# Spectral filter plus max-out experts on one core: wide exchange transfers through memory, filter rows doubled by TensorE, other loads held back in the opening

## The chip, the cores and the metric

One core of one Trainium2 chip runs the whole program. The metric is the device time of one execution in microseconds (us); runs of one kernel agree within about 1%. The profile of a kernel is one execution; its span is about 2 us shorter than the time.

Ratios are computed from the mean time of one kernel's fast runs over that of the other's of the same rounds, so a ratio is not quite the ratio of the medians that are quoted beside it.

## The reference

```python
# x: (8, 3072, 256) float32; filt_r, filt_i: (1537, 256); w1, w2: (256, 1024); w_out: (1024, 256)
X = np.fft.rfft(x, axis=1)
y = np.fft.irfft(X * (filt_r + 1j * filt_i)[None], n=3072, axis=1)   # a filter along the sequence
t = y.reshape(8 * 3072, 256)
out = np.maximum(t @ w1, t @ w2) @ w_out                             # the experts
```

## The kernel before

The transform of 3072 points is split as 128 x 24, and a batch of 3072 x 256 goes through these steps:

1. `gen_f1`: 12 matmuls with a 128 x 128 table (`C1`), evicted by ScalarE into `at` and stored to memory as `ad`.
2. `ad` is read back in another order as the *frequency tile* `bt` (96 partitions x 32 t x 256). This is the first exchange through memory.
3. `gen_f2`: for each of 16 pairs of t, a matmul with `U`, the product with the filter rows `F` on VectorE (`pqt`), four matmuls back (`pz`), eviction by ScalarE into `zt`, a store to `zd` (the *spectrum store*).
4. `zd` is read back as `zr` (128 partitions): the second exchange, called *read-back* below.
5. `s4` finishes the inverse transform; `moe_h` and `moe_o` are the experts. The maximum is rewritten as a ReLU of a difference of weights; that weight preparation (`prep_w`) is done once.

The experts of batch b run on TensorE while `gen_f2` of batch b+1 and `gen_f1` of batch b+2 are mixed in step by step. Before that can begin there is an *opening* that has nothing to hide behind: `gen_f1` and `gen_f2` of batch 0, `prep_w`, `gen_f1` of batch 1.

```python
    def copy_f(t0, t1):                       # the filter rows are needed twice, on partitions 0-47 and 48-95
        for ri in range(2):
            nc.sync.dma_start(out=F[48:96, ri, t0:t1], in_=F[0:48, ri, t0:t1])

    def load_f0():                            # 18 transfers of 1 to 12 rows, on the SyncE queue
        for ri, f in enumerate((filt_r, filt_i)):
            for dr in range(2):
                for mm, row0 in enumerate((0, 96) if dr == 0 else (32, 64)):
                    for q in range(2):
                        ...
    # ... (cut)
    # end of gen_f1: the frequency tile, 8 transfers over 24 partitions
                for h in range(2):
                    for rs in range(4):
                        src = ad[32 * rs + 16 * h:32 * rs + 16 * h + 16].rearrange("t n d -> n t d")
                        nc.sync.dma_start(out=bt_[24 * rs:24 * rs + 24, 16 * h:16 * h + 16], in_=src)
    # ... (cut)
    # gen_f2: the spectrum store, and at its end the read-back, 12 transfers over 32 partitions
            if g % 2 == 1:
                nc.sync.dma_start(out=zd[:, 2 * g - 2:2 * g + 2], in_=zt)
        # ...
        for g in list(range(2, 16)) + [0, 1]:
        # ...
        for c in range(3):
            for rs in range(4):
                src = zd[24 * rs + 8 * c:24 * rs + 8 * c + 8].rearrange("n t d -> t n d")
                nc.sync.dma_start(out=zr_[32 * rs:32 * rs + 32, 8 * c:8 * c + 8], in_=src)
    # ... (cut)
    # the opening
    drain(gen_f1(0))
    copy_f(1, 16)
    copy_f(16, 32)
    load_f0()
    load_w()
    for c in range(12):
        load_x(1, c)
    sines_u(uu, mk)
    tables_pe()
    f2 = gen_f2(0)
    # ... 16 steps of f2, prep_w(), drain(f2), drain(gen_f1(1)), loads of batch 2, s4(0)
```

(`load_f0` issues 18 transfers in all. The prediction and the expectations below say 28 small loads; that was a miscount.)

## Time and profile before

| | before |
|---|---|
| time, median (range) | 615.5 us (610.87 to 616.45) |
| first filter product (`pqt`) | 55.3 us |
| weight preparation begins (`w2b`) | 82.2 us |
| first expert matmul (`ph`) | 111.7 us |
| seventh tile's gap | 16.3 us, against 11.1 for its like six tiles later |
| from the sixth output store to the last | 416.2 us |

The page of the kernel before, its span and the mean busy share of the transfer engines in 40 equal slices (tenths):

```profile
span 613.5 us, 10246 instructions
DMA  8997529656976596658767785778336822261111
```

The stretches view: for each stretch its length, the busy us of TensorE (PE), its weight loads (PEld), VectorE (DVE), ScalarE (ACT), GpSimd (POOL), with the number of instructions in brackets, then the clock granted to TensorE, the transfer engines' share (the time of all packets over that of 16 engines; it can exceed 1), and GB/s:

```profile
0.00:20.00 20.00, 7.42 (x13) 1.27 (x13) 14.87 (x50) 8.99 (x15) 15.63 (x35) 1.00 0.93 155
20.00:40.00 20.00, 5.37 (x39) 3.83 (x39) 4.00 (x7) 9.57 (x20) 8.22 (x16) 1.00 1.22 201
40.00:60.00 20.00, 4.49 (x20) 3.87 (x21) 4.28 (x4) 1.19 (x2) 0.28 (x1) 1.00 0.87 167
60.00:80.00 20.00, 15.55 (x68) 12.25 (x67) 13.95 (x14) 5.45 (x11) 0.00 (x0) 1.00 0.48 158
80.00:100.00 20.00, 11.24 (x56) 7.03 (x54) 4.68 (x5) 9.08 (x16) 4.76 (x9) 0.92 0.53 99
100.00:120.00 20.00, 9.41 (x44) 5.11 (x45) 2.82 (x5) 7.99 (x15) 0.00 (x0) 0.57 0.82 205
200.00:220.00 20.00, 20.00 (x157) 15.29 (x156) 13.70 (x15) 13.32 (x25) 4.27 (x8) 1.00 0.65 154
```

The last line is the state of nearly all of the run: TensorE busy all the time, transfers at 0.65. The six lines above it are the opening, in which no engine is full. Who holds it up is in the waits view (engine and tile that waited, for what, us in total, times, longest):

```profile
DVE pqt L346 <- DMA F<-F: 23.5, 1, 23.5
ACT at L310 <- DMA ad<-at: 17.1, 3, 14.4
PE px L343 <- DMA bt__271<-ad: 15.3, 1, 15.3
ACT zt L335 <- DMA zd<-zt: 11.9, 2, 11.6
PE px L343 <- DMA bt__1412<-ad: 3.4, 1, 3.4
```

Read in order of time these are one chain: the frequency tile is late, then the doubled filter rows, then ScalarE has no free store buffer because stores are not issued, then the same again for the next transform. Why stores are not issued shows in the timeline of SyncE, which issues most transfers in program order (start, us, what, how many):

```profile
27.10 16.50 SPq L318 DMA_DIRECT2D bt__271<-ad  x8
43.72 7.84 SPq L102 DMA_DIRECT2D F<-F  x4
62.87 4.58 SPq L117 DMA_DIRECT2D F_96<-in_filt_i_dram  x6
68.62 22.49 SPq L337 DMA_DIRECT2D zd<-zt  x8
93.45 10.04 SPq L357 DMA_DIRECT2D zr__665<-zd  x12
103.83 7.65 SPq L312 DMA_DIRECT2D ad<-at  x6
```

The first product begins at 55.3 and ScalarE evicts it at 57.6, but the first store is issued at 68.6, behind the small filter loads; the stores of the next transform are issued at 103.8, behind twelve read-backs.

The output stores (start us, first column) mark the tiles. A tile is stored one tile later, so the time from the fifth store to the sixth is what TensorE spends on the seventh tile's first matmuls and the sixth's last ones; it is called the *seventh tile's gap* here. It is 16.3 us. The gaps repeat every six tiles, so its like is the gap of the thirteenth tile, 11.1 us:

```profile
174.56 0.54 POOL L416 DMA_DIRECT2D out_dram<-ot  x1 [7.72 <-DVE ot L412]
190.88 0.54 POOL L416 DMA_DIRECT2D out_dram<-ot  x1 [14.70 <-DVE ot L412]
242.51 0.53 POOL L416 DMA_DIRECT2D out_dram<-ot  x1 [7.73 <-DVE ot L412]
253.62 0.54 POOL L416 DMA_DIRECT2D out_dram<-ot  x1 [9.50 <-DVE ot L412]
```

### The profile page before, as it was taken

The page shows a single profiled execution, that of the slowest core. Times are in us where ns is not written, and L with a number is a line of the kernel's source. Part 1 is how long each engine was busy: PE and PEld are TensorE (multiplying, and loading weights), DVE is VectorE, ACT ScalarE, POOL GpSimd, SP SyncE. Part 2 cuts the span into 40 slices and gives each one's busy share as a digit, 9 for nine tenths or more (in the row PEclk, how much of TensorE's full clock was granted, in tenths as well). Part 3 has the DMA queues.
Part 4 walks back from the last instruction along what each step waited for, and adds up shares of the span by engine and source line. Part 5 has one row for each costly group of instructions (what it writes and reads, how often), then busy time and mean ns, then how long its engine had stood idle before and what let it go on. Part 6 is the DMA issues. An engine that isn't in the chain of part 4 may idle for free.

```text
span 613.5 us, 10246 instructions
## 1 busy us (share of the span) xinstructions
PE 536.0 (87%) x4008; PEld 395.0 (64%) x4008; DVE 335.0 (55%) x430; ACT 329.5 (54%) x588; POOL 86.0 (14%) x167
## 2 busy tenths in 40 slices
PE   3403771799979999999999999999999999999995
PEld 0203550477657777777777777777777777777774
DVE  8203740288337664666466637663667377734342
ACT  3801161566536754765476556765666455555541
POOL 8430002011111111111121102110000000000000
PEclk9999996699989999999999999999999999999998
DMA  8997529656976596658767785778336822261111
GB/s 140 208 188 148 180 62 219 171 123 169 225 182 156 134 220 198 153 152 183 212 150 179 163 218 145 183 156 233 125 112 161 225 83 78 74 185 70 69 69 69
DMA packets 90784, 94.62 MB, mean 154 GB/s; under 512 B 7360, under 2 KB 71504, under 8 KB 90592
## 3 DMA queue, kind: packets, MB, share of 16 engines
q1 hardware_dynamic: 66720, 54.17, 33.6%
q0 software_dynamic: 24016, 39.81, 28.5%
q8 instruction: 31, 0.51, 0.3%
q14 instruction: 17, 0.14, 0.1%
HBM read 56.72 MB, written 50.33 MB: 174 GB/s over the span
## 4 chain that ended last, share of the span: by engine, by line
PE 43%; issue 34%; DMA 12%; SPq 4%; POOL 3%; ACT 1%; DVE 1%; POOLq 0%; ACTq 0%
PE ph L385 14%; PE po L410 13%; PE po L405 3%; DMA xb<-in_x_dram 3%; PE pz L333 3%; PE px L343 3%; PE pz L334 3%; DMA Wo<-in_moe_w_out_dram 2%; DMA zd<-zt 2%; SPq L117 2%; POOL out_dram L416 2%; PE pa L309 2%; PE py L369 2%; DMA ad<-at 2%; DMA zr__665<-zd 1%
## 5 line engine op out<-in xcount | busy, mean ns | idle before, releaser
L410 PE MATMUL po<-Wo,gt 128*128 128x256 bf16 x1536 | 230.4, 273 | 0.0
L390 ACT ACTIVATE gt<-ph 128x512 bf16<-128x512 f32 x288 | 170.7, 593 | 100.4 <-PE ph L385 97.0
L346 DVE TENSOR_TENSOR pqt<-px,F 96x1024 bf16<-96x1024 f32 x128 | 156.0, 1219 | 107.6 <-PE px L343 83.6
L410 PEld LDWEIGHTS <-gt 128*128 128x128 bf16 x1536 | 150.2, 98 | 58.2
L335 ACT ACTIVATE zt<-pz 96x512 bf16<-96x512 f32 x128 | 75.3, 593 | 111.4 <-PE pz L334 87.9
L412 DVE COPY ot<-po 128x512 f32<-128x512 f32 x96 | 66.4, 692 | 75.8 <-PE po L410 75.8
L416 POOL DMA_DIRECT2D out_dram<-ot x48 | 25.8, 537 | 452.9 <-DVE ot L412 418.1
L385 PEld LDWEIGHTS <-Wd 128*128 128x128 bf16 x768 | 74.0, 99 | 19.5 <-issue 4.8
L310 ACT ACTIVATE at<-pa 128x512 bf16<-128x512 f32 x96 | 55.8, 597 | 54.0 <-PE pa L309 33.9
L388 DVE TENSOR_SCALAR gt<-ph 128x512 bf16<-128x512 f32 x96 | 65.5, 682 | 28.7 <-PE ph L385 28.7
L333 PE MATMUL pz<-pqt,VP 96*96 96x256 bf16 x256 | 67.9, 289 | 11.0 <-DVE pqt L346 10.7
L334 PE MATMUL pz<-pqt,VQ 96*96 96x256 bf16 x256 | 68.2, 290 | 0.0
L87 POOL DMA_DIRECT2D xb<-in_x_dram x96 | 51.4, 558 | 66.4 <-PE pa L309 50.4
L343 PEld LDWEIGHTS <-U 96*96 96x96 bf16 x256 | 32.5, 134 | 24.6 <-issue 22.9
L309 PE MATMUL pa<-xb,C_58 128*128 128x512 bf16 x96 | 38.3, 409 | 10.3 <-DMA xb<-in_x_dram 9.4
L334 PEld LDWEIGHTS <-VQ 96*96 96x96 bf16 x256 | 33.4, 130 | 13.2 <-issue 12.7
L333 PEld LDWEIGHTS <-VP 96*96 96x96 bf16 x256 | 33.7, 131 | 1.8 <-DVE pqt L346 1.1
L343 PE MATMUL px<-bt__271,U 96*96 96x256 bf16 x32 | 9.8, 416 | 18.3 <-DMA bt__271<-ad 15.3
L309 PEld LDWEIGHTS <-C_58 128*128 128x128 bf16 x96 | 9.5, 99 | 18.3 <-issue 7.5
L369 PE MATMUL py<-G_59,zr__665 128*128 128x128 bf16 x48 | 4.6, 248 | 14.6 <-ACT at L310 14.6
L369 PEld LDWEIGHTS <-zr__665 128*128 128x128 bf16 x48 | 3.9, 112 | 15.9 <-DMA zr__665<-zd 9.8
L374 DVE TENSOR_SCALAR y__760<-py 128x512 bf16<-128x512 f32 x1 | 0.7, 692 | 19.9 <-PE py L369 19.9
(334 smaller groups left out, 565.8 us busy)
## 6 DMA issues: line engine op xcount, KB each, us to landing
out_dram<-ot POOLq DMA_DIRECT2D x48, 512.0 KB, 3.9
xb<-in_x_dram POOLq DMA_DIRECT2D x96, 128.0 KB, 6.0
ad<-at SPq DMA_DIRECT2D x48, 256.0 KB
zd<-zt SPq DMA_DIRECT2D x64, 192.0 KB
bt__271<-ad SPq DMA_DIRECT2D x8, 192.0 KB
zr__665<-zd SPq DMA_DIRECT2D x12, 128.0 KB
bt__727<-ad SPq DMA_DIRECT2D x8, 192.0 KB
zr__1295<-zd SPq DMA_DIRECT2D x12, 128.0 KB
```

The source lines that it names most:

```text
L309: TE.matmul(pa, C1, xb[b, c], start=True, stop=True)
L310: S.activation(at[:, 2 * (c % 2):2 * (c % 2) + 2], pa, AF.Copy)
L333: TE.matmul(pz[:, i], VP[:, 2 * g + i], pqt[:, 0, i], start=True, stop=False)
L334: TE.matmul(pz[:, i], VQ[:, 2 * g + i], pqt[:, 1, i], start=False, stop=True)
L335: S.activation(zt[:, 2 * (g % 2):2 * (g % 2) + 2], pz, AF.Copy)
L343: TE.matmul(px[:, i], U[:, 2 * g + i].rearrange("p a b -> p (a b)"), bt_[:, 2 * g + i], start=True, stop=True)
L346: V.tensor_tensor(pqt, px.rearrange("p (o i) d -> p o i d", o=1).to_broadcast([QP, 2, 2, D]), F[:, :, 2 * g:2 * g + 2], OP.mult)
L385: TE.matmul(ph, Wd[:, dc, 128 * j:128 * j + 128], y_[:, dc].rearrange("p a b -> p (a b)"), start=(dc == 0), stop=(dc == 1))
L388: V.tensor_scalar(gt[tt][:, j], ph, 0.0, None, OP.max)
L390: S.activation(gt[tt][:, j], ph, AF.Relu)
L410: TE.matmul(p_, g_[:, jj, 128 * n:128 * n + 128], Wo[:, jj], start=False, stop=(jj == 7))
L412: V.tensor_copy(ot[tt][:, n - 1:n + 1], po[tt])
```

## The change

Its intent: lay out both exchanges so that they take few transfers over many partitions; take the doubling of the filter rows and the many small filter loads off the transfer queue; and hold back loads that the opening does not need. It also begins the products with t = 16 (whose filter rows are now loaded first), reads the spectrum back in two halves, the first of them in the middle of the tile, and gives four of batch 0's 16 products to GpSimd. For batch 0 it also lets two products wait for their matmuls back instead of one, and finishes the tile before the weight preparation. Cut to its core:

```diff
-        G.dma_start(out=t_, in_=src[:, 2 * c:2 * c + 2, :])        # 12 loads of 128 KB per batch
+        G.dma_start(out=t_, in_=src[:, 4 * c:4 * c + 4, :])        # 6 of 256 KB
 ...
-    def copy_f(t0, t1):
+    def copy_f(t0, t1, engine):
         for ri in range(2):
-            nc.sync.dma_start(out=F[48:96, ri, t0:t1], in_=F[0:48, ri, t0:t1])
+            for t in range(t0, t1, 2):
+                n = min(2, t1 - t)
+                pf = ps.tile([QP, 2, D], FP32, tag="ps", name="pf")
+                TE.matmul(pf[:, 0:n], DM, F[0:48, ri, t:t + n], start=True, stop=True)
+                ...  # evicted by VectorE or ScalarE into F[:, ri, t:t + n]
 ...  # load_f0: 4 loads at the start and 3 transfers later, instead of 18 small loads
-        S.activation(C1, uc.rearrange("p a b c -> p (a b c)"), AF.Sin, bias=zero, scale=TWO_PI)
+        S.activation(C1.rearrange("p (c a b) -> p a b c", a=2, b=2), uc, AF.Sin, bias=zero, scale=TWO_PI)
 ...
                 for h in range(2):
-                    for rs in range(4):
-                        src = ad[32 * rs + 16 * h:32 * rs + 16 * h + 16].rearrange("t n d -> n t d")
-                        nc.sync.dma_start(out=bt_[24 * rs:24 * rs + 24, 16 * h:16 * h + 16], in_=src)
+                    src = ad.rearrange("(t r) n d -> (r n) t d", r=4)[:, 16 * h:16 * h + 16]
+                    nc.sync.dma_start(out=bt_[:, 16 * h:16 * h + 16], in_=src)
 ...
-                nc.sync.dma_start(out=zd[:, 2 * g - 2:2 * g + 2], in_=zt)
+                nc.sync.dma_start(out=zd[2 * g - 2:2 * g + 2].rearrange("t p d -> p t d"), in_=zt)
+            if g == 15:
+                zr[b] = zrpool.tile([128, N2, D], BF16, tag="zr", name="zr")
+                read_z(1)
+            if g == 1:
+                read_z(0)
+        def read_z(h):
+            nc.sync.dma_start(out=zr[b][64 * h:64 * h + 64],
+                              in_=zd[16 * h:16 * h + 16].rearrange("t (r n) d -> (t r) n d", r=4))
-        for g in list(range(2, 16)) + [0, 1]:
+        for n, g in enumerate(list(range(8, 16)) + list(range(2, 8)) + [0, 1]):
 ...
+            if b == 0 and n in (1, 5, 9, 12):
+                E = G        # the product on GpSimd, from a copy in SBUF made by ScalarE
 ...  # the opening
     drain(gen_f1(0))
-    copy_f(1, 16)
-    copy_f(16, 32)
-    load_f0()
+    copy_f0()
     load_w()
-    for c in range(12):
-        load_x(1, c)
+    copy_f(16, 32, V)
     sines_u(uu, mk)
     tables_pe()
+    copy_f(2, 16, S)
+    copy_f(1, 2, S)
     f2 = gen_f2(0)
 ...  # inside the 16 steps: the last weight's load after step 1, batch 1's loads after steps 5 and 12
```

More of the change, by code (lines that the diff above doesn't have):

```diff
@@ L69 @@
     dram = ctx.enter_context(tc.tile_pool(name="dram", bufs=2, space=bass.MemoryType.DRAM))
-    xpool = ctx.enter_context(tc.tile_pool(name="xpool", bufs=16))
+    xpool = ctx.enter_context(tc.tile_pool(name="xpool", bufs=8))
     apool = ctx.enter_context(tc.tile_pool(name="apool", bufs=3))
@@ L76 @@
     pso = ctx.enter_context(tc.tile_pool(name="pso", bufs=2, space=bass.MemoryType.PSUM))
+    zrpool = ctx.enter_context(tc.tile_pool(name="zrpool", bufs=2))
     setup = ExitStack()
@@ L84, in load_x @@
     def load_x(b, c):
-        t_ = xpool.tile([128, 2, D], BF16, tag="xb", name="xb")
+        t_ = xpool.tile([128, 4, D], BF16, tag="xb", name="xb")
         src = x[b].rearrange("(p n) d -> p n d", n=N2)
-        G.dma_start(out=t_, in_=src[:, 2 * c:2 * c + 2, :])
+        G.dma_start(out=t_, in_=src[:, 4 * c:4 * c + 4, :])
         xb[b, c] = t_
@@ L98, in load_f @@
                 G.dma_start(out=F[24 * dr:24 * dr + 24, ri, t0:t1], in_=fsrc(f, row0, 64, 24, dt, t1 - t0))
-    def copy_f(t0, t1):
+    def copy_f(t0, t1, engine):
         for ri in range(2):
-            nc.sync.dma_start(out=F[48:96, ri, t0:t1], in_=F[0:48, ri, t0:t1])
+            for t in range(t0, t1, 2):
+                n = min(2, t1 - t)
+                pf = ps.tile([QP, 2, D], FP32, tag="ps", name="pf")
+                TE.matmul(pf[:, 0:n], DM, F[0:48, ri, t:t + n], start=True, stop=True)
+                if engine is V:
+                    V.tensor_copy(F[:, ri, t:t + n], pf[:, 0:n])
+                else:
+                    S.activation(F[:, ri, t:t + n], pf[:, 0:n], AF.Copy)
     F0 = init.tile([QP, 2, D], FP32)
@@ L109, in load_f0, with copy_f0 @@
             for dr in range(2):
-                for mm, row0 in enumerate((0, 96) if dr == 0 else (32, 64)):
-                    for q in range(2):
-                        p0 = 48 * q + 24 * dr + mm
-                        if p0 == 48:
-                            nc.sync.dma_start(out=F0[48:49, ri], in_=f[1536:1537, :])
-                            nc.sync.dma_start(out=F0[50:72:2, ri], in_=fsrc(f, 128, 128, J - 1, 1, 1))
-                        else:
-                            nc.sync.dma_start(out=F0[p0:p0 + 23:2, ri], in_=fsrc(f, row0, 128, J, 1, 1))
+                src = bass.AP(f.tensor, f.offset + 32 * dr * D, [[128 * D, J], [(96 - 64 * dr) * D, 2], [1, D]])
+                nc.sync.dma_start(out=F0[24 * dr:24 * dr + 24, ri], in_=src)
+    def copy_f0():
+        nc.sync.dma_start(out=F0[49:96], in_=F0[1:48])
+        nc.sync.dma_start(out=F0[48:49, 1], in_=filt_i[1536:1537, :])
+        nc.sync.dma_start(out=F0[48:49, 0], in_=filt_r[1536:1537, :])
+    DM = init.tile([48, QP], BF16)
     SW = init.tile([QP, QP], BF16)
@@ L121 @@
     zero = init.tile([128, 1], FP32)
+    V.memset(zero, 0.0)
     pid = init.tile([128, 1], FP32)
@@ L140 @@
            allow_small_or_imprecise_dtypes=True)
-    for c in range(12):
+    for c in range(6):
         load_x(0, c)
+    V.memset(DM, 0.0)
+    V.memset(I128, 0.0)
+    V.memset(SW, 0.0)
+    for b0 in (0, 48):
+        G.affine_select(out=DM, in_=DM, pattern=[[-1, QP]], compare_op=OP.not_equal,
+                        fill=1.0, base=b0, channel_multiplier=1)
+    G.affine_select(out=I128, in_=I128, pattern=[[-1, 128]], compare_op=OP.not_equal,
+                    fill=1.0, base=0, channel_multiplier=1)
+    G.affine_select(out=SW, in_=SW, pattern=[[-1, QP]], compare_op=OP.not_equal,
+                    fill=1.0, base=-48, channel_multiplier=1)
+    G.affine_select(out=SW, in_=SW, pattern=[[-1, QP]], compare_op=OP.not_equal,
+                    fill=-1.0, base=48, channel_multiplier=1)
     def table_c():
@@ L147, in table_c @@
         V.memset(kc[:, 1, 0, 0:1], 64.0)
-        V.memset(zero, 0.0)
         p128 = init.tile([128, 1], FP32)
@@ L157, in table_c @@
         V.tensor_tensor(uc, uc, rc, OP.subtract)
-        S.activation(C1, uc.rearrange("p a b c -> p (a b c)"), AF.Sin, bias=zero, scale=TWO_PI)
+        S.activation(C1.rearrange("p (c a b) -> p a b c", a=2, b=2), uc, AF.Sin, bias=zero, scale=TWO_PI)
     def tables_u():
-        V.memset(I128, 0.0)
-        G.affine_select(out=I128, in_=I128, pattern=[[-1, 128]], compare_op=OP.not_equal,
-                        fill=1.0, base=0, channel_multiplier=1)
-        V.memset(SW, 0.0)
-        G.affine_select(out=SW, in_=SW, pattern=[[-1, QP]], compare_op=OP.not_equal,
-                        fill=1.0, base=-48, channel_multiplier=1)
-        G.affine_select(out=SW, in_=SW, pattern=[[-1, QP]], compare_op=OP.not_equal,
-                        fill=-1.0, base=48, channel_multiplier=1)
         pq = pid[0:QP]
@@ L277, in load_w, with load_wo @@
         nc.sync.dma_start(out=w2f, in_=moe_w2.rearrange("(c p) j -> p c j", p=128))
+    def load_wo():
         G.dma_start(out=Wo, in_=moe_w_out.rearrange("(c p) j -> p c j", p=128))
@@ L308, in gen_f1 @@
             pa = ps.tile([128, 2, D], FP32, tag="ps")
-            TE.matmul(pa, C1, xb[b, c], start=True, stop=True)
+            TE.matmul(pa, C1, xb[b, c // 2][:, 2 * (c % 2):2 * (c % 2) + 2], start=True, stop=True)
             S.activation(at[:, 2 * (c % 2):2 * (c % 2) + 2], pa, AF.Copy)
@@ L323, in gen_f2 @@
         bt_ = bt[b]
-        zd = dram.tile([QP, T, D], BF16, tag="zd")
+        zd = dram.tile([T, QP, D], BF16, tag="zd")
         pend = []
@@ L345, in gen_f2 @@
             pqt = pqpool.tile([QP, 2, 2, D], BF16, tag="pq")
-            V.tensor_tensor(pqt, px.rearrange("p (o i) d -> p o i d", o=1).to_broadcast([QP, 2, 2, D]),
+            E = V
+            if b == 0 and n in (1, 5, 9, 12):
+                E = G
+                xs = init.tile([QP, 2, D], FP32, tag="xs", name="xs")
+                S.activation(xs, px, AF.Copy)
+                px = xs
+            E.tensor_tensor(pqt, px.rearrange("p (o i) d -> p o i d", o=1).to_broadcast([QP, 2, 2, D]),
                             F[:, :, 2 * g:2 * g + 2], OP.mult)
             pend.append((g, pqt))
-            if len(pend) > 1:
+            if len(pend) > (2 if b == 0 else 1):
                 s3(*pend.pop(0))
             yield
-        s3(*pend.pop(0))
-        zr_ = zrpool.tile([128, N2, D], BF16, tag="zr")
-        for c in range(3):
-            for rs in range(4):
-                src = zd[24 * rs + 8 * c:24 * rs + 8 * c + 8].rearrange("n t d -> t n d")
-                nc.sync.dma_start(out=zr_[32 * rs:32 * rs + 32, 8 * c:8 * c + 8], in_=src)
-        zr[b] = zr_
+        while pend:
+            s3(*pend.pop(0))
         yield
@@ L421, in drain @@
             pass
+    load_f0()
     table_c()
+    load_f(16, 32)
     load_f(1, 16)
-    load_f(16, 32)
     uu, mk = tables_u()
     drain(gen_f1(0))
-    copy_f(1, 16)
-    copy_f(16, 32)
-    load_f0()
+    copy_f0()
     load_w()
-    for c in range(12):
-        load_x(1, c)
+    copy_f(16, 32, V)
     sines_u(uu, mk)
     tables_pe()
+    copy_f(2, 16, S)
+    copy_f(1, 2, S)
     f2 = gen_f2(0)
-    for g in range(16):
-        if g == 13:
+    for n in range(16):
+        if n == 14:
             fix_f()
         next(f2)
+        if n == 1:
+            load_wo()
+        if n in (5, 12):
+            for c in range(3):
+                load_x(1, c + 3 * (n // 12))
+    drain(f2)
     prep_w()
     setup.close()
-    zrpool = ctx.enter_context(tc.tile_pool(name="zrpool", bufs=2))
     ypool = ctx.enter_context(tc.tile_pool(name="ypool", bufs=3))
@@ L446 @@
     opool = ctx.enter_context(tc.tile_pool(name="opool", bufs=2))
-    drain(f2)
     drain(gen_f1(1))
-    for c in range(12):
+    for c in range(6):
         load_x(2, c)
@@ L472 @@
                     next(f1, None)
-                c = (step - 3) // 2 - (5 if b == 0 else 0)
-                if b + 3 < B and step % 2 and 0 <= c < 12:
+                c = (step - 3 - (12 if b == 0 else 0)) // 4
+                if b + 3 < B and step % 4 == 3 and 0 <= c < 6:
                     load_x(b + 3, c)
```

## The prediction

> **What bounds the kernel now.** Two regimes. From about 187 to 604 us TensorE is busy in every 20 us stretch (stretches view: 20.00 of 20.00, clock 1.00); six output tiles take about 62.7 us (output stores). No transfer is on that path. From 0 to 111.7 us (first expert matmul, timeline) TensorE is mostly idle: 7.4, 5.4, 4.5, 15.6, 11.2, 9.4 us per 20 us. That opening is a chain of transfers. The waits view and the timeline name the links:
> - TensorE waits 15.3 us for the first frequency tile (46.0); VectorE idles 23.5 us until the filter rows doubled by SBUF-to-SBUF transfers arrive: first filter product at 55.3.
> - 28 small filter loads hold the transfer queue from 51.6 to 67.5. The first spectrum store is issued at 68.6; the store buffers fill, ScalarE waits 11.6 us, and the last pz is at 90.2.
> - Weight prep costs about 7 us (82.2 to 89.4), then 12 read-backs hold the queue from 93.4 to 103.5; the stores behind them cost ScalarE 14.4 us and TensorE 14.6 us.
> - Later, TensorE waits 3.4 us for a frequency tile at 174.5; that output tile takes 16.3 us against the usual 11.8: about 4.5 us lost.
> Transfers are saturated in the opening (share 0.93, then 1.22).
>
> **What the change does.** It removes 1.5 MB of doubling copies and 28 tiny loads. The second batch's and the last weight's loads (3.1 and 1.0 MB read) leave the window of the first tile. A frequency read becomes 2 transfers over 96 partitions instead of 8 over 24; a spectrum read-back 2 over 64 instead of 12 over 32. The Trainium skill (DMA: Bandwidth & Descriptors, "Why a DMA increments its semaphore by 16 and not by 1") takes as engine count the largest number up to 16 dividing the outer sizes: 12 for 24, 16 for 96. No view here shows engines singly. Rows of 512 B move from the spectrum read to its write.
> It adds 32 doubling matmuls, evicted by VectorE and ScalarE (0.69 and 0.59 us like those of that size: 11 and 9.5 us). Four products go to GpSimd; the Trainium skill (GPSIMD Engine Reference, "Elementwise — side-by-side cycle accounting") has it about 2x slower, so an estimated 2.5 us against VectorE's 1.22, hidden by the deeper pipeline. No run shows that yet.
>
> **New opening (estimates).** Frequency tile in at about 31; filter rows land at 20 to 28; doubling, table swaps (4.5 us VectorE) and doubling again are serial in TensorE's order: first product at about 41. Sixteen products at about 1.3 us (TensorE alone takes 1.28): last pz near 63. Weight prep 7, the second batch's transform 7 to 8 (12 evictions of 0.6), read-back hidden behind them: first expert matmul near 79 instead of 111.7. That is 33 us, all on the critical path, plus about 4 of the stall at 174.5. The rest stays.
>
> **Predicted: 579 us, range 569 to 594.** Chances: faster by over 2% 0.95, within 2% 0.04, slower by over 2% 0.01.
>
> **What would show it.** First product at 38 to 46 us; no filter-copy wait on VectorE; spectrum stores issued as they are made; first expert matmul at 73 to 87 us; no TensorE wait at the third batch's frequency read; six output tiles still in 62.7 us.
>
> **What would make it wrong.** Filter loads, still over 24 partitions, landing after 32 us and holding TensorE's in-order queue; GpSimd products over 4 us, stalling TensorE; second-batch loads issued late behind GpSimd work; 512 B stores slow enough to reach the TensorE-bound stage; a lower granted clock.

## The result, and the profile after

The median is 591.0 us (589.2 to 591.79), against 615.5; the ratio is 0.9612 (95% interval 0.9559 to 0.9666). All outputs are right. The time lies in the stated range, but 12 us above the middle of it: 24.5 us were gained where 36.5 were expected. Of the prediction's own six signs three failed: the spectrum stores were not issued as they were made, the first expert matmul came after 87 us, and TensorE still waits at the third batch's frequency read. The range was wide enough to take this in; these steps were not right.

| | before | after | predicted |
|---|---|---|---|
| first filter product | 55.3 | 40.8 | 41 (38 to 46) |
| last `pz` on TensorE | 90.2 | 62.6 | 63 |
| weight preparation begins | 82.2 | 70.4 | 63 |
| first expert matmul | 111.7 | 90.4 | 79 (73 to 87) |
| seventh tile's gap (11.1 without a stall) | 16.3 | 15.5 | about 12 |
| sixth output store to the last | 416.2 | 416.2 | unchanged |

The first expert matmul (`ph`) in the timelines of the kernel before and of the changed kernel:

```profile
111.67 4.43 PE L385 MATMUL ph<-y__760,Wd 128*128 128x512 bf16 x10 [1.86 <-ACT y__760 L372]
90.35 1.01 PE L408 MATMUL ph<-y__799,Wd 128*128 128x512 bf16 x2 [5.04 <-ACT y__799 L395]
```

The page of the changed kernel:

```profile
span 588.8 us, 9952 instructions
DMA  8998986688766955788378955794359324341112
```

The stretches view of the changed kernel, columns as above:

```profile
0.00:20.00 20.00, 6.59 (x14) 1.36 (x15) 15.17 (x51) 8.84 (x15) 13.27 (x30) 1.00 0.98 166
20.00:40.00 20.00, 19.24 (x72) 9.59 (x70) 13.58 (x23) 15.69 (x33) 0.00 (x0) 1.00 1.07 221
40.00:60.00 20.00, 15.21 (x86) 13.36 (x86) 14.45 (x13) 10.67 (x22) 12.46 (x11) 0.91 0.81 156
60.00:80.00 20.00, 10.18 (x55) 6.94 (x54) 4.41 (x5) 8.37 (x16) 2.97 (x7) 0.58 0.85 175
80.00:100.00 20.00, 11.29 (x62) 6.31 (x63) 3.36 (x5) 9.77 (x19) 0.40 (x1) 0.74 0.88 208
200.00:220.00 20.00, 19.84 (x155) 14.69 (x156) 8.73 (x12) 10.95 (x19) 1.21 (x3) 1.00 0.73 185
```

The opening's second and third stretches are now full of work, but from 60 to 90 us TensorE is half idle again, with the transfer engines at 0.85 and more. Its granted clock is 0.58 and 0.74 there, as it was 0.57 in the last stretch of the opening before. The steady state is as it was.

The waits view of the changed kernel. The wait for doubled filter rows is gone and the one for the first frequency tile too; three of the five are still there:

```profile
ACT at L324 <- DMA ad<-at: 11.1, 5, 4.6
ACT zt L348 <- DMA zd<-zt: 9.4, 2, 7.9
PE px L365 <- DMA bt__1429<-ad: 2.6, 1, 2.6
```

The first line adds up two transforms. In ScalarE's timeline 5.1 us of the 11.1 are waits in batch 0's transform, before 20 us, and 6.0 are waits in the next one's; the expectations below speak of the sum. In the kernel before, 14.4 of 17.1 us were the next transform's. The longest waits of each part:

```profile
15.70 2.23 ACT L324 ACTIVATE at<-pa 128x512 bf16<-128x512 f32 x4 [4.63 <-DMA ad<-at]
83.59 1.09 ACT L324 ACTIVATE at<-pa 128x512 bf16<-128x512 f32 x2 [3.00 <-DMA ad<-at]
87.38 1.09 ACT L324 ACTIVATE at<-pa 128x512 bf16<-128x512 f32 x2 [2.71 <-DMA ad<-at]
```

The timeline of SyncE shows why the wait for spectrum stores is still there. The early read-back (`zr`, 58.39) sits in the order of the queue between the fourth and the fifth spectrum store. SyncE may not issue it before the four stores have landed, so nothing is issued from 53.2 to 58.4, and the fifth store goes out at 59.02:

```profile
26.24 1.09 SPq L331 DMA_DIRECT2D bt__274<-ad  x2
45.99 7.23 SPq L350 DMA_DIRECT2D zd<-zt  x4
58.39 0.54 SPq L358 DMA_DIRECT2D zr<-zd  x1
59.02 11.86 SPq L350 DMA_DIRECT2D zd<-zt  x4
73.16 0.47 SPq L358 DMA_DIRECT2D zr<-zd  x1
78.66 11.50 SPq L326 DMA_DIRECT2D ad<-at  x6
```

The output stores around the seventh tile of the changed kernel:

```profile
152.71 0.54 POOL L439 DMA_DIRECT2D out_dram<-ot  x1 [7.72 <-DVE ot L435]
168.25 0.54 POOL L439 DMA_DIRECT2D out_dram<-ot  x1 [14.46 <-DVE ot L435]
```

The stall costs 15.5 - 11.1 = 4.4 us, of which 2.6 are the wait. The rest coincides with a lower granted clock after it: 0.66 from 155 to 160 us, where `h1_first` below, without the wait, has 1.00.

The two spans differ by 24.7 us, and it adds up: 21.3 to the first expert matmul, 0.5 to the first output store, 0.8 in the seventh tile's gap, 0 from the sixth to the last output store (416.23 in both), 2.1 between the last store's issue and the end of the execution. So the questions are which parts made the 21, why it was not 33, and why the seventh tile's stall stayed.

### The profile page after: what moved, and what is told of

It reads as the page before. It is cut to its first block, busy times and chain, and to the rows that moved or that the text cites. A ratio compares the mean times of both kernels' runs of the same rounds, so it can differ in the third digit from the quotient of the medians.

```text
span 588.8 us, 9952 instructions
## 1 busy us (share of the span) xinstructions
PE 539.2 (92%) x3971; PEld 397.4 (67%) x4040; DVE 340.9 (58%) x443; ACT 339.5 (58%) x608; POOL 70.9 (12%) x125
## 2 busy tenths in 40 slices
DMA packets 76514, 93.07 MB, mean 158 GB/s; under 512 B 4595, under 2 KB 56357, under 8 KB 75396
## 4 chain that ended last, share of the span: by engine, by line
PE 54%; issue 28%; DMA 11%; DVE 2%; POOL 2%; ACT 2%; SPq 0%; POOLq 0%; ACTq 0%
PE po L433 18%; PE ph L408 15%; PE po L428 5%; DMA ad<-at 4%; PE pz L346 4%; PE px L365 4%; PE pz L347 3%; DMA zd<-zt 3%; PE pa L323 3%; PE py L392 2%; DMA bt__1429<-ad 2%; DMA bt__784<-ad 2%; POOL out_dram L439 1%; ACT at L324 1%; DVE F L109 1%
## 5 line engine op out<-in xcount | busy, mean ns | idle before, releaser
L413 ACT ACTIVATE gt<-ph 128x512 bf16<-128x512 f32 x288 | 170.6, 594 | 99.4 <-PE ph L408 95.5
L374 DVE TENSOR_TENSOR pqt<-px,F 96x1024 bf16<-96x1024 f32 x124 | 151.0, 1220 | 88.3 <-PE px L365 88.0
L433 PEld LDWEIGHTS <-gt 128*128 128x128 bf16 x1536 | 150.1, 98 | 58.4 <-issue 0.6
L348 ACT ACTIVATE zt<-pz 96x512 bf16<-96x512 f32 x128 | 75.5, 592 | 81.5 <-PE pz L347 59.6
L346 PE MATMUL pz<-pqt,VP 96*96 96x256 bf16 x256 | 65.9, 283 | 5.0 <-POOL pqt L374 4.3
L347 PE MATMUL pz<-pqt,VQ 96*96 96x256 bf16 x256 | 66.1, 283 | 0.0
L323 PE MATMUL pa<-xb,C_58 128*128 128x512 bf16 x96 | 37.1, 411 | 9.3 <-DMA xb<-in_x_dram 8.6
L392 PE MATMUL py<-G_59,zr 128*128 128x128 bf16 x384 | 29.8, 221 | 3.2 <-ACT at L324 3.2
L392 PEld LDWEIGHTS <-zr 128*128 128x128 bf16 x384 | 25.8, 98 | 5.0 <-issue 3.9
L88 POOL DMA_DIRECT2D xb<-in_x_dram x48 | 26.2, 561 | 17.0 <-PE pa L323 16.8
L323 PEld LDWEIGHTS <-C_58 128*128 128x128 bf16 x96 | 9.4, 100 | 15.8 <-issue 6.6
L107 PE MATMUL pf<-F,DM 48*96 48x512 bf16 (+1 forms) x32 | 14.1, 611 | 4.9 <-ACT at L324 4.6
L107 PEld LDWEIGHTS <-DM 48*96 48x96 bf16 x32 | 5.9, 190 | 13.1 <-issue 13.1
```

The source lines that it names most:

```text
L323: TE.matmul(pa, C1, xb[b, c // 2][:, 2 * (c % 2):2 * (c % 2) + 2], start=True, stop=True)
L346: TE.matmul(pz[:, i], VP[:, 2 * g + i], pqt[:, 0, i], start=True, stop=False)
L347: TE.matmul(pz[:, i], VQ[:, 2 * g + i], pqt[:, 1, i], start=False, stop=True)
L348: S.activation(zt[:, 2 * (g % 2):2 * (g % 2) + 2], pz, AF.Copy)
L374: E.tensor_tensor(pqt, px.rearrange("p (o i) d -> p o i d", o=1).to_broadcast([QP, 2, 2, D]), F[:, :, 2 * g:2 * g + 2], OP.mult)
L392: TE.matmul(py[:, n], zr[b][:, 4 * i + n, 128 * dc:128 * dc + 128], G1, start=True, stop=True)
```

## The experiments

All are edits of the changed kernel but `only_layouts`, which edits the kernel before. Twelve kernels were run, in four rounds on four chips, beside the kernel before (medians 613.5 to 614.5 us) and not beside the changed kernel. Its 591.0 us is of an earlier round (before: 615.5), so a difference of 2 us or less from 591.0 shows nothing.

### Which part made the gain

**The old exchange layouts in the changed kernel** (`old_layouts`).

```diff
-        S.activation(C1.rearrange("p (c a b) -> p a b c", a=2, b=2), uc, ...)
+        S.activation(C1, uc.rearrange("p a b c -> p (a b c)"), ...)
 # the 8 frequency reads, the [96, 32, 256] order of zd and the 12 read-backs at the end as before
```

> The changed kernel with the exchange layouts of before (8 frequency reads over 24 partitions, spectrum stores in 2 KB rows, 12 read-backs over 32 partitions at the end). Theory A, the wide layouts carry a large part of the gain: the first expert matmul moves from 90.4 to beyond 100 us and the time goes back to 603 us or more. Theory B, the gain comes from what was taken out of and moved around in the opening (filter doubling, small filter loads, held loads) and the layouts are worth little: first expert matmul within 4 us of 90.4, time 586 to 597 us.

Measured: 600.04 us median, ratio to before 0.9799 (0.9742 to 0.9855). The first expert matmul came at 89.0, not later than the changed kernel's 90.4, and the weight preparation began at 64.0. The loss lies after the opening: the first tile took 22.2 us to its output store against 18.0, and the seventh tile's gap was 21.7 against 15.5. Neither theory had this: going back costs about 9 us on the medians (11.5 by the ratios), all of it after the first expert matmul. But this edit also takes away the early read-back of the changed kernel, which cost time by itself. `readback_last` below has the new layouts with both read-backs at the end, and its first expert matmul came at 86.2; against that kernel the old layouts cost about 3 us in the opening too.

**The new layouts alone** (`only_layouts`).

```diff
 # in the kernel before: C1's columns, the 2 frequency reads, zd as [32, 96, 256], and
-        for c in range(3):
-            for rs in range(4):
-                ...                                              # 12 read-backs
+        for h in (1, 0):
+            nc.sync.dma_start(out=zr_[64 * h:64 * h + 64],
+                              in_=zd[16 * h:16 * h + 16].rearrange("t (r n) d -> (t r) n d", r=4))
```

> The kernel before with the new exchange layouts alone, nothing else moved. Theory A: first expert matmul falls from 111.7 to below 101 us, time 605 us or less. Theory B: first expert matmul at 106 to 113 us, time 608 to 617 us; the read-back's hold on the queue (10 us with 12 transfers) gets shorter, but the waits for the doubled filter rows and the 28 small loads stay.

Measured: 605.76 us, ratio 0.9878 (0.9841 to 0.9915): 8.3 us on the medians. First expert matmul at 105.4 (between the two theories), and the seventh tile's gap fell from 16.3 to 12.4. So the layouts alone gave 8.3 us, and all the rest without the layouts 14.0 (614.07 to 600.04); the two sum to 22.3, near the whole of 24.5. Here, with the products still beginning with t = 4, the layouts did remove most of the seventh tile's stall (12.4 against 11.1 without one), which the full change did not. That was the hint for `h1_first` below.

**The doubling by transfers again** (`dma_doubling`).

```diff
+    copy_f(16, 32, V)   # now two transfers F[48:96] <- F[0:48]; right behind the frequency tile
+    copy_f(1, 16, S)
     copy_f0()
     load_w()
-    copy_f(16, 32, V)
     sines_u(uu, mk)
     tables_pe()
-    copy_f(2, 16, S)
-    copy_f(1, 2, S)
```

> The changed kernel with the filter rows doubled by SBUF-to-SBUF transfers again, queued right behind the first frequency tile and ahead of the small filter copies and weights. If the doubling by TensorE is on the path to the first product as the prediction had it: first product moves from 40.8 to 47 us or later, time plus 6 us or more (597 or more). Rival: with the other loads held back the four copies land by 40 us anyway and TensorE, VectorE and ScalarE are freed of 32 matmuls and evictions: first product at 42 us or earlier, time within 3 us of 591.

Measured: 595.87 us, ratio 0.9713 (0.9669 to 0.9758), so the doubling on TensorE is worth about 5 us. But the first product came at 40.4, not later: the rival was right on that, since with the other loads held back the four copies arrive in time. The cost came after it. SyncE issued the 2 MB of the first two weights at 42.0 instead of 33.4, just ahead of the spectrum stores; ScalarE waited 11.3 us for store buffers (9.4 in the changed kernel), so its copy for GpSimd's third product was late, and TensorE waited 9.4 us for GpSimd's products (4.3). That the weights slowed the stores fits the order but was not tried by itself. The first expert matmul came at 93.2 (2.8 later), and in the profiled run one read-back was late in the steady state (the twelfth tile's gap was 12.1 us against 8.3).

**The other loads not held back** (`loads_early`).

```diff
     load_w()
+    load_wo()
+    for c in range(6):
+        load_x(1, c)
     copy_f(16, 32, V)
 ...
-        if n == 1:
-            load_wo()
-        if n in (5, 12):
-            for c in range(3):
-                load_x(1, c + 3 * (n // 12))
```

> The changed kernel with the loads of the second batch and of the last weight issued where the kernel before had them, ahead of the filter doubling. If holding them back pays: filter rows or frequency tile later, first product after 43 us, time 595 us or more. Rival: the opening is now bound by compute (doubling, table swaps) and not by transfers, and loads issued late are what slows the stores after 50 us: first product within 2 us of 40.8, spectrum stores faster, ScalarE's store waits under 3 us instead of 9.4, time 583 to 590 us.

Measured: 590.73 us, ratio 0.9651 (0.9597 to 0.9705): the time of the changed kernel (591.0). Both theories were half right. VectorE's timeline of this run: the first product came 6 us later, at 46.8, because TensorE waited 6.0 us for the frequency tile:

```profile
46.76 2.35 DVE L374 TENSOR_TENSOR pqt<-px,F 96x1024 bf16<-96x1024 f32 x2 [12.70 <-PE px L365]
```

And yet the weight preparation began at 70.5 (70.4 in the changed kernel) and the first expert matmul came at 90.1. ScalarE's wait for spectrum stores fell from 9.4 to 0.8 us. Holding the loads back brings the first product forward by 6 us and gives the 6 us back at the stores, which then run beside the loads that were held. That the loads slow the stores is read from this pair of runs; what share of the 9.4 us they make was not separated from the place of the early read-back (`readback_last` below).

**All products on VectorE** (`no_gpsimd`).

```diff
-            if b == 0 and n in (1, 5, 9, 12):
+            if False:
```

> The changed kernel with all 16 products of the first tile on VectorE again. The prediction had the four GpSimd products as hidden and worth little: time within 2 us of 591 and first expert matmul within 2 us of 90.4. Rival: VectorE was the bound there, the products take 1.3 us longer per product moved: first expert matmul 3 us or more later, time 594 or more.

Measured: 591.58 us, ratio 0.9646 (0.9609 to 0.9684); first expert matmul at 91.3. As expected, but the run is not the clean test it was meant to be. With no product to wait for on GpSimd's in-order queue, the last weight's load was issued at 15.9 us and the second batch's loads from 19.9 us on: nothing else in the program holds them back. The first product then came at 50.5, with TensorE waiting 9.5 us for the frequency tile. So it is `loads_early` and the product's place changed together, and again the end is the same. Put beside `loads_early`, whose loads went out at nearly the same times (15.8 and 19.6), it says something of the products: from the first product to the last `pz` it took 19.6 us with all of them on VectorE, 22.9 in `loads_early` and 21.8 in the changed kernel. The four products on GpSimd did not shorten this stretch. (The GpSimd product took 2.11 us in the changed kernel, VectorE's 1.22.)

### Why the seventh tile's stall stayed

**The frequency read as eight transfers again** (`bt_pieces`), with the new order in memory.

```diff
                 for h in range(2):
-                    src = ad.rearrange("(t r) n d -> (r n) t d", r=4)[:, 16 * h:16 * h + 16]
-                    nc.sync.dma_start(out=bt_[:, 16 * h:16 * h + 16], in_=src)
+                    for rs in range(4):
+                        src = ad.rearrange("(t r) n d -> r n t d", r=4)[rs][:, 16 * h:16 * h + 16]
+                        nc.sync.dma_start(out=bt_[24 * rs:24 * rs + 24, 16 * h:16 * h + 16], in_=src)
```

> The changed kernel with each frequency read as 8 transfers over 24 partitions again, from the new layout in memory; all else as changed. If covering 16 engines is what made the layouts pay (old layouts: seventh tile's gap 21.7 us against 15.5): the read takes over 12 us and that gap grows to 19 us or more, time 595 or more. Rival: the gain of the layouts is that 12 read-backs no longer hold the queue in front of the transform's stores: gap within 1.5 us of 15.5, time within 2 us of 591.

Measured: 608.61 us, ratio 0.9907 (0.9846 to 0.9969). This undoes most of the change with one loop. Its four runs spread more than the others' (605.1, 606.0, 611.2, 612.4), and the profile is of the longest. The seventh tile's gap was 18.5 (expected 19 or more), the first expert matmul 95.0. Of the 21.8 us by which its span is longer, 11.1 are in the steady state, where TensorE now waits for read-backs in four places that never waited before. Its line in the waits view:

```profile
PE py L393 <- DMA zr<-zd: 7.3, 4, 2.8
```

How many engines a transfer used can be counted. Each engine that takes part ends with one small write to the completion semaphore, says the Trainium skill (DMA: Bandwidth & Descriptors, "Why a DMA increments its semaphore by 16 and not by 1"), and the engine count is the largest number up to 16 that divides the outer sizes of both sides. Then 8 transfers over 24 partitions should make 8 x 12 small writes, and 2 over 96 partitions 2 x 16; over 8 batches the difference is 512. The packet lines of the changed kernel and of this one, in this order:

```profile
DMA packets 76514, 93.07 MB, mean 158 GB/s; under 512 B 4595, under 2 KB 56357, under 8 KB 75396
```

```profile
DMA packets 77027, 93.08 MB, mean 152 GB/s; under 512 B 5107, under 2 KB 56869, under 8 KB 75908
```

5107 - 4595 = 512, exactly. The trace's records of the 3072 packets of 512 B of the second batch's frequency read give what it costs. (The records' clock is set so that the last one ends with the span; it may be off by 1 us.)

```
kernel          transfers           first packet  half   last    first to last
before          8 x 24 partitions      116.1      120.4  125.2    9.1 us
old_layouts     8 x 24                  94.2       98.7  104.1    9.9
bt_pieces       8 x 24                  99.2      103.7  108.8    9.6
only_layouts    2 x 96                 112.3      115.7  119.5    7.2
after           2 x 96                  94.6       98.1  102.2    7.6
combined        2 x 96                  92.4       95.9   99.9    7.5
```

A packet took 39 to 41 ns on average in all six. 3072 packets of 40 ns are 10.2 us on 12 engines and 7.7 us on 16, an estimated difference of 2.6 us a batch; measured, the means of the three narrow and the three wide reads differ by 2.1. That the eight narrow transfers also occupy SyncE for 5.0 us where two take 1.4 (third batch's read) goes with it; which of the two makes the read-backs late was not separated. Also open: why narrow reads from the new order in memory cost more (608.6) than narrow reads, stores and read-backs from the old one (600.0).

**The half that is needed first, first** (`h1_first`).

```diff
-                for h in range(2):
+                for h in (1, 0):
                     src = ad.rearrange("(t r) n d -> (r n) t d", r=4)[:, 16 * h:16 * h + 16]
```

> The changed kernel with the two halves of each frequency read issued in the other order, the half with t 16 to 31 first. The change makes the products begin with t 16, but still reads t 0 to 15 first, so the first product waits for the whole read; before, it began with t 4 and needed only the first half. If that mismatch is why the later stall stayed: TensorE's 2.6 us wait at the third batch goes and the seventh tile's gap falls from 15.5 to 13 us or less, time 2 to 4 us lower (587 to 589). Rival: the whole read is late for other reasons (contention, queue order): gap within 1 us of 15.5, time within 1.5 us of 591.

Measured: 585.32 us, ratio 0.9546 (0.9503 to 0.9588), 5.7 us below the changed kernel's median and 4.1 us below it by the ratios: at or past the upper end of the expected 2 to 4 us. TensorE's wait for the third batch's tile is gone from its waits, and the output stores of this run show the seventh gap at 11.1 us:

```profile
152.13 0.54 POOL L439 DMA_DIRECT2D out_dram<-ot  x1 [7.72 <-DVE ot L435]
163.24 0.54 POOL L439 DMA_DIRECT2D out_dram<-ot  x1 [10.03 <-DVE ot L435]
```

So the stall stayed because the change turned round the order of the products (t from 16) but not that of the read (t from 0). In the kernel before, the first product needed half of the read: the half point in the table above comes 4.3 us after the first packet. In the changed kernel it needed all of it, 7.6 us, and the gain in width was lost again. The profiled opening was a little shorter as well: ScalarE's store wait was 3.2 instead of 9.4 and the first expert matmul came at 89.1; the first product was at 40.9 as before, and why the stores did better is not shown.

**The third batch's transform earlier** (`f1_early`).

```diff
                         next(f2, None)
-                        if step % 2:
+                        if step < 24:
                             next(f1, None)
```

> The changed kernel with the third batch's first transform put into steps 12 to 23 of the first expert round instead of every second step to 35. It gives the frequency read about 12 steps (15 us) more. If the later stall (15.5 us for the seventh tile against 11.8) is only that read landing late: the seventh tile's gap falls to 12 us or less, time 3 to 4 us lower (587 to 588). Rival: the stall is contention or the queue order and moves elsewhere, for example to the second batch's stores in the same steps: sum of the first six gaps unchanged, time within 1.5 us of 591.

Measured: 591.45 us, ratio 0.9632 (0.9597 to 0.9666): no gain. The seventh tile's gap fell to 11.5, but the sixth tile's grew from 8.3 to 12.8 us, because TensorE now waited 4.0 us for the second batch's read-back. The gaps from the first to the sixth store sum to 60.3 us, against 59.9. As the rival had it, the stall moved: SyncE issued the frequency read at 133.1, ahead of three spectrum stores (134.2 to 140.2), two of which had been free to go since 126.8 and 130.1, and the read-back behind them went out at 148.6 instead of 133.9.

### Why the opening was 11 us longer than predicted

**Both read-backs at the end of the tile** (`readback_last`).

```diff
-            if g == 15:
-                zr[b] = zrpool.tile([128, N2, D], BF16, tag="zr", name="zr")
-                read_z(1)
             if g == 1:
+                zr[b] = zrpool.tile([128, N2, D], BF16, tag="zr", name="zr")
+                read_z(1)
                 read_z(0)
```

> The changed kernel with both halves of the spectrum read-back issued at the end of the tile, none in its middle. Theory H, the early read-back waits in the in-order transfer queue for its stores to land (SyncE held from 53.2 to 58.4) and blocks the stores behind it, so ScalarE runs out of store buffers: ScalarE's store wait falls from 9.4 to under 3 us, the weight prep starts at 62 to 65 instead of 70.4, first expert matmul at 80 to 86 instead of 90.4, time 582 to 588 us. Rival S, 512 B stores are slow and the loads issued late beside them slow them: the store waits stay above 6 us and the prep starts after 68.

Measured: 589.14 us, ratio 0.9593 (0.956 to 0.9626). ScalarE's wait for spectrum stores is gone, and the weight preparation begins at 64.1 instead of 70.4. This is theory H, and it shows that the early read-back, not the size of the rows, made the 7.9 us wait. The run takes away its hold on SyncE and its own 768 KB, which moved ahead of the fifth store, at once; the two were not separated. Nor is its place enough alone: in `loads_early` it stands in the same place and ScalarE waits 0.8 us. Little of it reached the end. ScalarE's wait for the next transform's stores grew from 6.0 to 7.8 (with batch 0's, from 11.1 to 13.3), the first expert matmul came 4.2 us earlier, at 86.2, and the seventh tile's gap grew by 1.5. The time missed the expected 582 to 588, and is too near 591.0 to be called a gain.

**Six spectrum store buffers instead of three** (`z_buffers`).

```diff
-    zpool = ctx.enter_context(tc.tile_pool(name="zpool", bufs=3))
+    zpool = ctx.enter_context(tc.tile_pool(name="zpool", bufs=6))
 # room from a scratch tile of the tables, used for one half after the other:
-        ru = init.tile([QP, 2, T, 2, J, 2], FP32)
+        ru = init.tile([QP, T, 2, J, 2], FP32)
```

> The changed kernel with 6 spectrum store buffers instead of 3 (room made by halving one table scratch tile of the setup), read-back order as changed. Both H and S say that ScalarE's store wait nearly goes (under 2 us) and the weight prep starts at 61 to 65. Under H the queue still holds up the stores, so the last read-back is issued after 70 us all the same and the first transform's stores behind it; first expert matmul 83 to 88 us. Were the store wait not on the path at all, the time would stay at 591.

Measured: 587.13 us, ratio 0.9551 (0.9517 to 0.9586). The store wait is gone, the preparation begins at 64.9, and the first expert matmul comes at 88.1 (expected 83 to 88). The time is 3.9 us lower on the medians, 3.7 by the ratios. The last read-back is still issued at 73.5, as expected, and the transform's stores follow 0.5 us behind its 768 KB: ScalarE waits 9.9 us for them at once (6.0 in the changed kernel).

**The third batch's loads later** (`x2_later`).

```diff
     drain(gen_f1(1))
-    for c in range(6):
-        load_x(2, c)
     s4(0)
 ...
+                if b == 0 and step < 6:
+                    load_x(2, step)
```

> The changed kernel with the third batch's six loads issued in the first six steps of the first expert round (about 92 us on) instead of from 60 us on, as soon as their buffers come free. Theory T, the opening up to the first expert matmul is now bound by transfer work (the engines' share is 0.98, 1.07, 0.81, 0.85, 0.94), so what is issued in it sets its length: spectrum stores land faster, ScalarE's waits for stores (9.4 and 11.1) fall by half or more together, first expert matmul at 80 to 86 us, time 581 to 587 us. Rival Q, the waits come from the in-order queue alone: first expert matmul within 2 us of 90.4, time within 2 us of 591.

Measured: 589.2 us, ratio 0.9617 (0.9568 to 0.9666). Theory T was too simple: with these loads out of the opening the first expert matmul came at 89.2, 1.2 us earlier. The store waits were 5.7 us and, in the next transform, 7.0, where 9.4 and 6.0 had been: 2.7 less together, not half. These loads are not what fills the last part of the opening.

**Put together** (`combined`).

```diff
 # h1_first, x2_later, the halved scratch tile, and
-    xpool ... bufs=8      apool ... bufs=3      zpool ... bufs=3
+    xpool ... bufs=7      apool ... bufs=6      zpool ... bufs=4
```

> The changed kernel with the needed half of the frequency read first, the third batch's loads after the first expert matmul, 4 spectrum store buffers and 6 transform store buffers (room from the halved scratch tile and one load buffer fewer). If ScalarE's waits for store buffers are the last link before the experts (9.4 plus 11.1 us in the changed kernel): both waits under 4 us together, first expert matmul at 81 to 86 us, seventh tile's gap 11 to 13 us, time 578 to 584 us. If instead the transfers themselves are the limit there, the wait only changes its name: first expert matmul at 87 us or later, time 584 to 587, no better than with the half order alone (585.3).

Measured in five rounds: 580.77 us (579.53 to 581.92), ratio to before 0.9459 (0.9432 to 0.9486). This beats both kernels. First expert matmul at 81.5, seventh tile's gap 11.1, both waits of ScalarE for store buffers gone: all inside what the first theory expected. So the waits for buffers, which moved from store to store in the runs before, held the opening. That the transform's six buffers did most is argued and not shown: they were never run alone. The three parts that were run by themselves (`h1_first`, `x2_later`, and more spectrum buffers in `z_buffers`) brought the first expert matmul forward by 1.3, 1.2 and 2.3 us, together less than the 8.9 here. The stores themselves did not get faster (the longest landing of one was 12.2 us, against 7.8 in the changed kernel), but with six buffers ScalarE goes on without them. What is left of the wait is on TensorE, before the first expert matmul (4.9 us for the read-back, at 80.1) and after it (3.4 us for the second batch's frequency tile, at 95.5). So of the 8.9 us only 4.8 are left at the first output store (103.5 against 108.3); most of the rest of the gain over the changed kernel is the seventh tile's 4.4. The first expert matmul, and the waits view of this run:

```profile
81.48 3.93 PE L408 MATMUL ph<-y__787,Wd 128*128 128x512 bf16 x10 [0.38 <-ACT y__787 L395]
PE py L392 <- DMA zr<-zd: 5.1, 2, 4.9
PE px L365 <- DMA bt__784<-ad: 3.4, 1, 3.4
```

## Why the prediction was right or wrong, point by point

- **Two regimes, and the gain in the opening: right.** 21.3 of 24.7 us of span came before the first expert matmul; from the sixth output store to the last both kernels took 416.23 us.
- **"No transfer is on that path": right for a gain, too bold for a loss.** `bt_pieces` made four waits for read-backs in the steady state by making one transfer slower. TensorE was full there, but with little slack behind it.
- **First product at about 41: right (40.8), but the doubling was not what set it.** By transfers, with the loads held back, it came at 40.4; with the doubling on TensorE and the loads early at 46.8. With the rest of the change in place, either of the two takes most of the way from 55.3 (with both undone it was not run). On the time they differ: the doubling on TensorE is worth 5 us, the holding back nothing (590.7 against 591.0).
- **"Last pz near 63": right for TensorE** (62.6; it then waits 8.9 us until 71.55), **but ScalarE's evictions ended 8 us later, at 70.6.** The step "spectrum stores issued as they are made" failed. They were blocked by the early read-back, which the prediction counted as free ("read-back hidden behind them"). `readback_last` and `z_buffers` each start the preparation 5.6 to 6.4 us earlier.
- **"The second batch's transform 7 to 8 (12 evictions of 0.6)": mis-sized.** It took 12.7 us (77.1 to 89.8, TensorE's first of them to ScalarE's last), of which ScalarE waited 6.0 us for its own stores. The term counted the evictions and not the three buffers behind them. Together with the point before (preparation begun at 70.4 instead of 63), these 5 us make up the 11 us between 79 and 90.4. `combined`, which gives both steps buffers, has 81.5.
- **"Plus about 4 of the stall at 174.5": wrong.** 0.8 us of it went, of the 5.2 that it cost (16.3 against 11.1). The prediction costed the width of the read and overlooked that the products now begin with the half that is read last. `h1_first` shows it: one swapped loop removes the whole stall (gap 11.1).
- **A frequency read covers 16 engines instead of 12: right as the skill states it**, counted as 512 fewer small writes, and worth 2 us per frequency read.
- **GpSimd's products hidden: not quite.** 2.11 us each, 1.7 times VectorE's 1.22; TensorE waited 4.3 us for the four together. Beside `loads_early`, `no_gpsimd` ran the products' stretch 3.2 us faster without them, and the times agree (590.7 and 591.6), so no gain of theirs is shown; what they are worth with the loads held back stays open.
- **The small filter loads (18 of them, not 28) were not undone by themselves.** That they held the queue from 51.6 to 67.5 is read from the profile before; their own share of the 14 us that came without the layouts was not measured.

## What to carry to other kernels

When a consumer's order is turned round, turn the order of its transfers round too: a read that is 2 us shorter gains nothing if its first user now waits for the last piece. On an in-order issuing queue, a transfer that waits for earlier stores to land stops everything behind it, so place it where nothing behind it is urgent, or give the producer enough buffers to run through. In a stretch where several engines take turns, removing one wait moves it to the next link (loads, stores, read-back); change the links together, and judge by when the stretch ends, not by when its first step begins.

## What the Trainium skill lacked or had wrong

- DMA: Bandwidth & Descriptors, "Why a DMA increments its semaphore by 16 and not by 1", gives the rule for the number of engines and was exact here (512 small writes), but this section gives no cost for a transfer on fewer engines: 1.5 MB in rows of 512 B took 9.1 to 9.9 us on 12 engines (eight transfers) and 7.2 to 7.6 on 16 (two).
- The same page, "Rules for kernel authors", tells to wait for the first transfer's semaphore before issuing one that reads its data. These rules do not say that the wait also holds all later transfers of that issuing engine: 5.2 us of silence on SyncE here, and the next step began 6.4 us earlier with the read-back moved to the end.
- The same rules advise against splitting a transfer over disjoint partitions, and say nothing of splitting it along the free dimension so that a consumer can start on the first part. The order of two such halves was worth 4 to 6 us.
- GPSIMD Engine Reference, "Elementwise — side-by-side cycle accounting", has GpSimd about 2 times slower than VectorE for an operation on two tensors. Here a product of 96 x 1024 took 2.11 us from SBUF against 1.22 us from PSUM on VectorE, 1.7 times.
